# One head group per lap of TensorE's loop, kept values in the third slot, and a 28 KB ring for the weights between two layers

## The chip, the cores and the metric

The kernel runs on one core of a Trainium2 chip. TensorE (PE) multiplies matrices, VectorE (DVE), ScalarE (ACT) and GpSimd (POOL) do the rest, and SyncE (SP) issues nearly all DMAs. The core has 16 DMA engines, which serve one queue here. The metric is the device time of one execution in microseconds, the median over several.

## The reference

Two identical decode blocks follow each other, with the same weights and the same caches:

```
x = x + attention(layernorm(x))        # 2 batches, 1 query position, 512 channels
x = x + reglu(layernorm(x))            # twice, for two layers

attention: q = x @ wq                  # 32 query heads of 128
           scores = q . k_cache / sqrt(128)   # 8 key/value heads, 32768 positions
           p = softmax(scores); o = p @ v_cache; return o @ wo
reglu:     h = relu(x @ W_gate) * (x @ W_up); return h @ W_down     # 1792 hidden channels
```

All is float32. Each of the 16 pairs of batch and key/value head ("head group") has 16.8 MB of keys and 16.8 MB of values, and both layers read them all. The weights of one layer are 27.8 MB.

## The kernel before

A head group's keys and its values come as two halves each (`half`), 128 partitions by 32 blocks of 512 columns, 8.39 MB. They lie in three slots of 32 blocks in one SBUF tensor, `arena`, taken in turn (`slot`). For each block of keys `k_blocks` issues a matmul of the four query rows, padded with zeros to 32 columns (`qz`), into `pair`; for each block of values `v_blocks` issues one into `acc`. `soft_max` and `soft_tail` make the probabilities and their transpose between the two. `head_out` turns the sum of one group into columns of `oT`, and after each second group `project` multiplies by a part of `wo` (1 MB) and adds to `op`.

The order of work is written out by hand: `keys(i)` and then `values(i - 1)`, so that the softmax of group i has its keys' time and values' time to run in. Each engine works its list in order; a recorder (`Tape`) finds, for each operation, what it must wait for from the regions of `arena` and the other tensors, and sets semaphores. A load is issued by SP as soon as TensorE has used what lay at its place; loads behind it in SP's list wait with it. TensorE's list is long, so for groups 2 to 13 its instructions stand in a hardware loop of two groups a lap (`LOOPED`, `laps`); the other engines' lists are written out in full.

The second layer takes the head groups in reverse. So the last group of the first layer is the first of the second, and what is still in SBUF isn't loaded again: its two key halves and the first half of its values (`kept`), which fill the three slots.

With the slots full, all that crosses the border flows through three strips of 2048 columns behind them (`strip`): the second half of the last values (`FLOWN`), the last part of `wo`, then `wgu` (gate and up weights) in 8 loads of 896 KB, `wd` (down weights) in 6 loads, and the second layer's `wq` in 8 loads of 1 MB. `feed_forward` and `queries` do this work. The strips also hold, at other times, `wo` (`WO_AT`), the softmax's probabilities (`P_AT`), and the scaled sums (`ACS_AT`). In `queries` of the second layer the scores of the kept keys are made between the weights' matmuls, eight blocks at a time, and the next group's keys follow in three pieces (`EASED`).

At the end of the second layer the last values come in six pieces (`ENDING`), and `wo`, `wgu` (4 loads of 1.75 MB) and `wd` are loaded into free slots well before their use. The result, `xq`, is stored as 128 rows.

The profile's lines all name line 179, where the recorder calls the instruction; groups are told apart by their tiles.

Of the kernel before, what the change touches and what calls it, by code (L numbers as in the profile page):

```python
# [36 lines left out]
WO_AT, ACS_AT, MT_AT, P_AT = FLOW, FLOW + STRIP, FLOW + STRIP + D, FLOW + STRIP + 1024  # L37
PT_AT = (FLOW + 2 * STRIP, OWN)
WIDE_AT, XT_AT, SQ_AT = OWN, OWN + D, OWN + D + P
DOWN = (4, 4, 2, 2, 1, 1)  # L40
# [4 lines left out]
ENDING = ((32, 48), (48, 56), (56, 58), (58, 60), (60, 62), (62, 64))  # L45
# [8 lines left out]
class Tape:  # L54
# [28 lines left out]
    def add(self, engine, call, args, kw):  # L83
        lane = kw.pop("lane", None)
# [3 lines left out]
        ins = [a for a in (*args[1:], *kw.values()) if isinstance(a, bass.AP) and not any(a is o for o in outs)]  # L88
# [29 lines left out]
        loop = self.spot if engine == "tensor" else None  # L118
        for k, (n, other) in sorted(needs.items(), key=lambda x: -len(x[1][1].clock)):
            if loop is not None or known.get(k, 0) < n:  # L120
                op.waits[k] = n
                for e, m in ((k, n), *other.clock.items()):
                    known[e] = max(known.get(e, 0), m)
# [18 lines left out]
    def write(self):  # L142
# [66 lines left out]
        nc.sync.wait_ge(sems["out"], 16)  # L209
# [59 lines left out]
def attention_reglu_decode(nc, hold, x, k, v, wq, wo, wgu, wd, consts, out):  # L269
# [13 lines left out]
    qz = sbuf("qz", 2 * QZ).rearrange("p (a b) -> p a b", b=QZ)  # L283
# [16 lines left out]
    turn = [0, 2, 0, 0]  # L300
# [5 lines left out]
    def own(i, at):  # L306
        e = 32 + 8 * (i % 2) + 2 * at
        return stat[:, e : e + 1]

    def slot():  # L310
        turn[1] += 1
        return (turn[1] - 1) % SLOTS * ROW

    def strip():
        turn[2] += 1
        return FLOW + (turn[2] - 1) % STRIPS * STRIP

    def fetch(at, src, lane=None):
        t = arena[:, at : at + src.shape[-1]]
        if lane is None:  # L320
            lane = f"lane{turn[3] % LANES}"
            turn[3] += 1
        sp.dma_start(t, src, lane=lane)
        return t

    def half(src, n, h):
        at = slot()
        return at, fetch(at, src[n, h], f"slot{at // ROW}" if tape.spot else None)

    def spans(src, n, at, parts):  # L330
        for lo, hi in parts:
            e = at(lo) if callable(at) else at + (lo % HALF) * D
            yield lo, hi, fetch(e, src[n, lo // HALF, :, lo % HALF * D : (lo % HALF + hi - lo) * D])
# [7 lines left out]
    dve.memset(op, 0.0)  # L341

# [36 lines left out]
    def queries(L, total, first, between):  # L379
        xT, ss = centred(total)  # L380
        qp = pair2[0]
# [3 lines left out]
        if L == 0:  # L385
            whole = fetch(slot(), wq)
        for e, b in enumerate(order):
            B, kt = divmod(b, KT)
            w = fetch(strip(), wq[:, b * 4 * D : (b + 1) * 4 * D]) if L else whole[:, b * 4 * D : (b + 1) * 4 * D]
            for c in range(4):  # L390
                pe.matmul(qp[32 * c : 32 * c + 32, B, :], xT[:, kt, :], w[:, c * D : (c + 1) * D],
                          start=kt == 0, stop=kt == KT - 1)
# [4 lines left out]
            if kt == KT - 1:  # L397
                q = tile(WIDE_AT, D)
                qs = q.rearrange("p (a b) -> p a b", b=32)
                dve.transpose(q, qp[:, B, :])  # L400
                for n in range(NB):
                    dve.tensor_scalar_mul(qT[:, 16 * B : 16 * B + 16, n], qs[:, :, n], rq[:, n : n + 1])
                if B == front:
                    place_queries(0, first)

    def place_queries(i, n):
        hk, b = divmod(n, NB)
        dve.tensor_copy(qz[:, i % 2, 28 : 28 + REP], qT[:, REP * hk : REP * hk + REP, b])

    def scores(i):  # L410
        return pair2[(i + 1) % 2]

    def k_blocks(i, lo, kt):
        for at in range(kt.shape[-1] // D):
            j, ch = divmod(lo + at, 8)
            B, c = divmod(ch, 4)
            pe.matmul(scores(i)[32 * c : 32 * c + 32, B, :], qz[:, i % 2, 28 - 4 * j : 60 - 4 * j],
                      kt[:, at * D : (at + 1) * D], start=j == 0, stop=j == NT - 1)

    def soft_max(i):  # L420
        m1, nm, rs = own(i, 0), own(i, 1), own(i, 2)
# [7 lines left out]
    def soft_tail(i):  # L429
        pT, p = tile(PT_AT[i % 2], 2 * D), tile(P_AT, 2 * D)  # L430
        for B in range(2):
            dve.transpose(pT[:, B * D : (B + 1) * D], p[:, B * D : (B + 1) * D])
        pe.matmul(small[1][:, 0:1], same, own(i, 2), start=True, stop=True)
        dve.reciprocal(own(i, 3), small[1][:, 0:1])

    def v_blocks(i, lo, hi, vt, first, last):
        pT = tile(PT_AT[i % 2], 2 * D).rearrange("p (b m r) -> p b m r", m=16, r=32)
# [12 lines left out]
    def evacuate(i, split=False):  # L450
        acs = tile(PT_AT[i % 2] if split else ACS_AT, D)
        w = P if split else D
        for t in range(0, D, w):
            dve.tensor_scalar_mul(acs[:, t : t + w], acc[:, t : t + w], own(i, 3))
        return acs

    def head_out(acs, n):
        for t in range(4):
            pe.matmul(small[0][:, :REP], acs[:, t * P : (t + 1) * P], selh[:, 4 * t : 4 * t + 4], start=t == 0, stop=t == 3)
        dve.tensor_copy(oT[:, :, n % NB], small[0][:, :REP])  # L460

    def project(w, final, closing=False):
        for u in range(REP):
# [3 lines left out]
            else:  # L467
                pe.matmul(op[32 * u : 32 * u + NB, :], oT[:, u, :], rows, start=False, stop=closing)
# [6 lines left out]
    def feed_forward(L, total, ends):  # L475
        xT, ss = centred(total)
        gu = pair2[1]
        gh, hT = tile(WIDE_AT, FS), tile(XT_AT, FS)
        per = 2 if ends else 1
        for s in range(2):  # L480
            for kt in range(KT):
                b = s * KT + kt
                if b % per == 0:
                    t = fetch(ends[0] + b * F if ends else strip(), wgu[:, b * F : (b + per) * F])
                w = t[:, b % per * F : (b % per + 1) * F]
                for j in range(4):
                    pe.matmul(gu[32 * j : 32 * j + 32, s, :FS], xT[:, kt, :], w[:, j * FS : (j + 1) * FS],
                              start=kt == 0, stop=kt == KT - 1)
                if b == 0:
                    rs = factor(ss, True)  # L490
            if s == 0:
# [8 lines left out]
        for n in DOWN:  # L500
            if ends:
                at = ends[1] + c * D
            elif n == 4 or c in (8, 12):
                at = begun = strip()
            else:
                at = begun + n * D
            t = fetch(at, wd[:, c * D : (c + n) * D])
            for e in range(n):
                w = t[:, e * D : (e + 1) * D]
                if n == 4:  # L510
                    pe.matmul(dn[32 * e : 32 * e + 32, :], rows[:, c + e, :], w, start=c == 0, stop=c == 4)
                else:
                    spread(tot, rows[:, c + e, :], w, c + e == 8, c + e == NC - 1)
# [10 lines left out]
    kept = []  # L524
    for L in range(NLAYER):
        last = L == NLAYER - 1
        seq = list(range(NG)) if L % 2 == 0 else list(range(NG - 1, -1, -1))
        made = {}

        def keys(i):  # L530

            if i < NG - 1:
                place_queries(i + 1, seq[i + 1])
            at = 0
            for h in range(2):
                if last and i == 1 and h == 0:
                    parts = ((lo, t) for lo, hi, t in spans(k, seq[i], slot(), EASED))
                else:
                    parts = [(HALF * h, half(k, seq[i], h)[1])]
                for lo, t in parts:  # L540
                    for e in range(0, t.shape[-1] // D, 8):
                        k_blocks(i, lo + e, t[:, e * D : (e + 8) * D])
                        at += 1
                        if at == 2 and 1 <= i < NG - 1:
                            soft_tail(i - 1)
                        if at == 3 and i >= 2:
                            if i < NG - 1:
                                head_out(made.pop(i - 2), seq[i - 2])
                            if i % 2 == 1:
                                project(fetch(WO_AT, wo[seq[i - 2] // NB], "wo"), False, i == NG - 1)  # L550
                            if i == NG - 1:
                                head_out(made.pop(i - 1), seq[i - 1])
                                combine()
                if last and i == 1 and h == 0:
                    v_blocks(0, 0, HALF, kept[2], True, False)

        def values(i, soft):
            n = seq[i]
            for h in range(2):
                if last and i == 0 and h == 0:  # L560
                    continue
                t = half(v, n, h)[1]
                for e in range(0, HALF, 8):
                    v_blocks(i, HALF * h + e, HALF * h + e + 8, t[:, e * D : (e + 8) * D], h == e == 0, HALF * h + e == 56)
                    if soft is not None and e == 0 and h == (1 if last and i == 0 else 0):
                        soft_max(soft)
                    if i == NG - 2 and h == 0 and e == 8:
                        head_out(made.pop(i - 1), seq[i - 1])
            made[i] = evacuate(i)

        def kept_scores():
            for e in range(0, 64, 8):
                k_blocks(0, e, kept[e // HALF][:, e % HALF * D : (e % HALF + 8) * D])
                yield

        first = kept_scores() if last else iter(())
# [98 lines left out]
```

## Time and profile before

| What | Value |
|---|---|
| median of 3 runs | 2580.14 us (2574.63 to 2581.72) |
| the profiled execution | 2578.07 us, of which its span is 2576.3 us |
| TensorE busy | 51% of the span, mean granted clock 0.746 |
| VectorE, ScalarE, GpSimd busy | 6%, 2%, 0% |
| moved by DMA | 1104.94 MB, on average 429 GB/s |

How to read the lines that follow: a group line has the engine, the operation, output <- inputs, partitions x elements and how often (x), then busy time and the mean of one. A timeline line begins with start and duration in us; in brackets at its end stand the idle time before it and what ended it. A line of the chain of work that ended last has start, duration and what the time was spent on. PEld is TensorE's load of the stationary side. Every float32 matmul and its load appear as two instructions.

### The profile page before, as it was taken

Reading aid. Unit: us, or ns where it says so; the run is one execution under the profiler, and the core shown is the slowest. Engines: PE = TensorE matmul, PEld = TensorE weight load, DVE = VectorE, ACT = ScalarE, POOL = GpSimd, SP = SyncE. Lnnn points to the kernel's source line nnn. Section 1 sums busy time; section 2 is a strip of 40 time slices with the busy share of each in tenths; the row PEclk is TensorE's granted clock in tenths of the full one; section 3 lists DMA queues with packets and bytes.
Section 4 is the critical chain, followed back from the end, with each engine's and each line's share of the span. In section 5 each row is a group of like instructions: output and inputs, shape, how many; then the busy total and the mean of one; then the engine's idle time right before and its main releaser. Section 6 shows DMA issues by size and latency. Waiting matters only on the chain.

```text
span 2576.3 us, 19494 instructions
## 1 busy us (share of the span) xinstructions
PE 1308.5 (51%) x9224; PEld 333.7 (13%) x9224; DVE 147.6 (6%) x359; ACT 41.1 (2%) x67; POOL 3.0 (0%) x11
## 2 busy tenths in 40 slices
PE   2554554454455445544675455445445545554456
PEld 0111111111111111111111111111111111111111
DVE  0000000000000000000011000000000000000001
ACT  0000000000000000000000000000000000000000
POOL 0000000000000000000000000000000000000000
PEclk9777777777777777777778777777777777777777
DMA  9999999999999999999999999999999999999998
GB/s 425 425 435 438 431 431 437 431 433 432 427 440 434 431 433 430 437 434 432 403 367 434 436 429 434 434 432 435 434 430 436 430 430 439 433 432 431 433 434 368
DMA packets 27972, 1104.94 MB, mean 429 GB/s; under 512 B 3104, under 2 KB 3488, under 8 KB 6304
## 3 DMA queue, kind: packets, MB, share of 16 engines
q1 hardware_dynamic: 27648, 1104.23, 99.7%
q8 instruction: 30, 0.49, 0.1%
q10 hardware_dynamic: 288, 0.17, 0.0%
q14 instruction: 6, 0.05, 0.0%
HBM read 1104.32 MB, written 0.07 MB: 429 GB/s over the span
## 4 chain that ended last, share of the span: by engine, by line
DMA 76%; PE 20%; another core or an unknown queue 2%; SPq 1%; DVE 0%; issue 0%; ACT 0%; ACTq 0%; DVEq 0%
DMA arena<-k 44%; DMA arena<-v 27%; PE pair L179 13%; PE acc L179 5%; DMA arena<-wgu 2%; DMA cst<-consts 2%; PE small L179 1%; DMA arena<-wq 1%; SPq L179 1%; PE op L179 1%; DMA arena<-wd 0%; DMA arena<-wo 0%; DVE arena L179 0%; DVE oT L179 0%
## 5 line engine op out<-in xcount | busy, mean ns | idle before, releaser
L179 PE MATMUL acc<-arena 128*16 128x512 f32 (+1 forms) x4120 | 584.8, 723 | 603.2 <-DMA arena<-v 602.6
L179 PE MATMUL pair<-arena,qz 128*32 128x512 f32 x4096 | 596.1, 736 | 573.8 <-DMA arena<-k 573.8
L179 PEld LDWEIGHTS pair<-arena,qz 128*32 128x32 f32 x4096 | 140.7, 132 | 987.1 <-DMA arena<-k 628.8
L179 PEld LDWEIGHTS acc<-arena 128*16 128x16 f32 x4120 | 119.5, 109 | 1017.3 <-DMA arena<-v 537.5
L179 DVE TENSOR_REDUCE stat<-pair 128x1 f32<-128x1024 f32 x32 | 39.2, 1225 | 652.9 <-PE pair L179 652.9
L179 ACT ACTIVATE arena<-pair,stat 128x1024 f32<-128x1024 f32 (+1 forms) x34 | 36.9, 1086 | 2447.4 <-DVE stat L179 2364.1
L179 DVE TENSOR_SCALAR arena<-acc,stat 128x512 f32<-128x512 f32 (+1 forms) x38 | 24.8, 665 | 756.2 <-PE acc L179 756.2
L179 PE MATMUL pair<-arena 128*32 128x512 f32 (+1 forms) x256 | 44.4, 805 | 21.4 <-DMA arena<-wgu 11.5
L179 DVE STREAM_TRANSPOSE arena<-arena 128x512 f32<-128x512 f32 (+1 forms) x68 | 43.2, 671 | 5.1 <-ACT arena L179 4.9
L179 PEld LDWEIGHTS small<-cst,arena 128*128 128x128 f32 x256 | 31.2, 191 | 27.7 <-issue 25.2
L179 PE MATMUL small<-cst,arena 128*128 128x4 f32 x256 | 34.0, 256 | 1.1 <-DVE arena L179 1.1
L179 DVE RECIPROCAL stat<-small 128x1 f32<-128x1 f32 x32 | 5.2, 163 | 387.9 <-PE small L179 387.9
L179 PE MATMUL small<-stat,ones 128*128 128x2 f32 x16 | 4.5, 349 | 45.1 <-DVE stat L179 45.1
L179 DVE TENSOR_REDUCE stat<-small 128x1 f32<-128x32 f32 x32 | 6.1, 192 | 358.6 <-PE small L179 358.6
L179 PE MATMUL small<-arena,cst 128*128 128x32 f32 (+1 forms) x80 | 18.0, 342 | 7.0 <-DVE arena L179 7.0
L179 PEld LDWEIGHTS small<-arena,cst 128*128 128x128 f32 (+1 forms) x80 | 13.5, 227 | 56.7 <-issue 45.4
L179 PE MATMUL op<-arena,oT 128*2 128x512 f32 (+1 forms) x176 | 17.2, 491 | 5.3 <-DVE oT L179 4.5
L179 PE MATMUL small<-stat,cst 128*128 128x1 f32 x64 | 12.4, 264 | 3.0 <-ACT arena L179 3.0
L179 PEld LDWEIGHTS small<-stat,cst 128*128 128x128 f32 x64 | 9.7, 191 | 29.9 <-issue 26.6
L179 PEld LDWEIGHTS pair<-arena 128*32 128x32 f32 x256 | 7.2, 130 | 47.3 <-DMA arena<-wgu 24.3
L179 DVE COPY oT<-small 128x4 f32<-128x4 f32 x32 | 5.2, 163 | 140.2 <-PE small L179 140.2
L179 PE MATMUL small<-arena 128*32 128x128 f32 (+1 forms) x128 | 11.0, 486 | 3.4 <-DMA arena<-wd 2.1
(40 smaller groups left out, 56.0 us busy)
## 6 DMA issues: line engine op xcount, KB each, us to landing
arena<-wo SPq DMA_DIRECT2D x16, 1024.0 KB, 50.6
arena<-v SPq DMA_DIRECT2D x2, 4096.0 KB, 44.8
arena<-wq SPq DMA_DIRECT2D x8, 1024.0 KB, 7.5
arena<-v SPq DMA_DIRECT2D x7, 1024.0 KB, 6.3
arena<-wgu SPq DMA_DIRECT2D x8, 896.0 KB, 6.1
arena<-wgu SPq DMA_DIRECT2D x4, 1792.0 KB, 36.5
arena<-v SPq DMA_DIRECT2D x3, 2048.0 KB, 48.6
arena<-wd SPq DMA_DIRECT2D x4, 1024.0 KB, 18.8
```

Source lines behind the costliest of these rows:

```text
L179: ins = getattr(engine, op.call)(*op.args, **op.kw)
```

## The change

- TensorE's loop holds one head group a lap: groups 1 to 14 in the first layer, 2 to 15 in the second. So that every lap has the same instructions, there is one query buffer `qz`, one place for the transposed probabilities, one score buffer for all groups but the first, and `project` runs in each lap: `head_out` clears the other batch's columns of `oT` before it, and its copy into `oT` waits for the load of `wo` too. `nothing` opens and closes the sum in `op` with zeros.
- The slots X, Y, Z have fixed uses. In the first layer keys go to X and Y and values to Z and Y; in the second keys to Y and X and values to Z and X. The last groups of a layer are placed by hand.
- The last values of the first layer go to Z and the strips' area, and their last pieces to the front of Z again, over blocks already used (`FLOWN`). Both key halves stay in Y and X, and 30 blocks of values stay in Z (`KEPT`); the other 34 are loaded again (`AGAIN`).
- The weights at the border flow through one ring of 7168 columns (28 KB a partition: the strips' area and the last 1024 columns of Z). Pieces are 2 x 448 columns of `wgu` (448 KB, 16 of them), 1024 columns of `wd` (512 KB, six and two halves) and of `wq` (512 KB, 16 of them).
- At the end of the second layer `wgu` comes in pieces of 8, 8, 8, 4 and 4 units of 448 columns.
- `queries` gathers in `acc` and `op` instead of `pair`. The result is stored as 4 rows for each of the two batches, one store on SP and one on ACT.

The diff, cut to its core:

```diff
-SLOTS = 3
-FLOW = SLOTS * ROW
-STRIP = 2048
-STRIPS = 3
+X, Y, Z, FLOW = 0, ROW, 2 * ROW, 3 * ROW
-OWN = FLOW + STRIPS * STRIP
+OWN = FLOW + 6144
-LOOPED = range(2, 14)
-KEPT = ((0, 16), (16, 24), (24, 32))
-FLOWN = tuple((32 + 4 * e, 36 + 4 * e) for e in range(7)) + ((60, 62), (62, 64))
+RING = FLOW - 1024, OWN
+WO_AT = FLOW + 2048
+P_AT, ACS_AT, MT_AT = WO_AT + 2048, WO_AT + 3072, WO_AT + 3584
+PT_AT = WIDE_AT = OWN
+LAPS = range(1, 15), range(2, 16)
+FLOWN = ((0, 2, 32, Z), (0, 0, 2, RING[0]), (1, 0, 12, FLOW), (1, 12, 20, Z), (1, 20, 28, Z + 8 * D),
+         (1, 28, 30, Z + 16 * D), (1, 30, 32, Z + 18 * D))
+KEPT = ((54, 64, Z + 10 * D), (44, 54, Z), (22, 32, Z + 20 * D))
+AGAIN = ((0, 0, 22, Z), (1, 0, 12, Z + 22 * D))
+UNITS = (2,) * 16, (8, 8, 8, 4, 4)
+DOWN = (2,) * 6 + (1, 1), (4, 4, 2, 2, 1, 1)
...
-    def strip():
-        turn[2] += 1
-        return FLOW + (turn[2] - 1) % STRIPS * STRIP
+    def ring(width):
+        at = turn[1] if turn[1] + width <= RING[1] else RING[0]
+        turn[1] = at + width
+        return at
...
+                if L and c % 2 == 0:
+                    w = fetch(ring(2 * D), wq[:, at : at + 2 * D])
...
+    def head_out(n, w=None, acs=tile(ACS_AT, D)):
...
+        if w is not None:
+            dve.memset(oT[:, :, 1 - n % NB], 0.0)
+        dve.tensor_copy(oT[:, :, n % NB], small[0][:, :REP], also=() if w is None else (w,))
...
+    def nothing(start):
+        for u in range(REP):
+            pe.matmul(op[32 * u : 32 * u + NB, :], qz[:, :NB], mean_cols.to_broadcast([P, D]), start=start, stop=not start)
...
+            if e in begins:
+                n = begins[e]
+                t, at = fetch(X + e * FS if last else ring(n * FS), wgu[:, e * FS : (e + n) * FS]), e
...
+            t = fetch(Y + c * D if last else ring(n * D), wd[:, c * D : (c + n) * D])
...
+        k_at, v_at = ((X, Y), (Z, Y)) if not last else ((Y, X), (Z, X))
...
+                if h == 1 and tape.spot and i % 2 == 0 and i > 0:
+                    weights[0] = out_weights(i)
...
+        def lap(i):
+            for at in keys(i):
+                if at == 2:
+                    soft_tail()
+                if at == 3:
+                    head_out(seq[max(i - 2, 0)], weights[0])
+                    project(weights[0])
+            values(i - 1, i)
...
+            for e, (h, lo, hi, at) in enumerate(AGAIN):
+                t = part_of(v, seq[0], h, lo, hi, at)
+                if e == 0:
+                    weights = [out_weights(0)]
+                    soft_max(1)
+                    place_queries(seq[2])
+                v_blocks(HALF * h + lo, HALF * h + hi, t, False, e == len(AGAIN) - 1)
...
+        for i in tape.laps(LAPS[L], 1):
+            lap(i)
...
+            for e, (h, lo, hi, at) in enumerate(FLOWN):
+                t = part_of(v, n, h, lo, hi, at)
+                v_blocks(HALF * h + lo, HALF * h + hi, t, e == 0, e == len(FLOWN) - 1)
...
-    sp.dma_start(out, xq, lane="out")
+    for b, queue in enumerate((sp, act)):
+        queue.dma_start(out[:, b, :], bass.AP(xq.tensor, xq.offset + b * P, [[32 * P, 4], [1, P]]), lane=f"out{b}")
```

More of the change, by code (lines that the diff above doesn't have):

```diff
@@ L87, in add @@
         outs = [args[0]] + [kw[k] for k in ("accum_out",) if k in kw]
-        ins = [a for a in (*args[1:], *kw.values()) if isinstance(a, bass.AP) and not any(a is o for o in outs)]
+        ins = [a for a in (*args[1:], *kw.values(), *also) if isinstance(a, bass.AP) and not any(a is o for o in outs)]
         key = lane or engine
@@ L118, in add @@
         loop = self.spot if engine == "tensor" else None
+        here = {}
         for k, (n, other) in sorted(needs.items(), key=lambda x: -len(x[1][1].clock)):
-            if loop is not None or known.get(k, 0) < n:
+            if (known if loop is None else here).get(k, 0) < n:
                 op.waits[k] = n
+                here.update({e: max(here.get(e, 0), m) for e, m in other.clock.items()})
                 for e, m in ((k, n), *other.clock.items()):
@@ L208, in write @@
                 done = {}
-        nc.sync.wait_ge(sems["out"], 16)
+        for b in range(NB):
+            nc.sync.wait_ge(sems[f"out{b}"], 16)
         nums = sorted(s.num for s in sems.values())
@@ L380, in queries @@
         xT, ss = centred(total)
-        qp = pair2[0]
+        qp = acc, op
         rq = one()
@@ L499, in feed_forward @@
         c = 0
[L500 to L511, printed above, removed]
+        for n in DOWN[last]:
+            t = fetch(Y + c * D if last else ring(n * D), wd[:, c * D : (c + n) * D])
+            for e in range(c, c + n):
+                w = t[:, (e - c) * D : (e - c + 1) * D]
+                if e < 8:
+                    g = 32 * (e % 4)
+                    pe.matmul(dn[g : g + 32, :], rows[:, e, :], w, start=e < 4, stop=e >= 4)
                 else:
-                    spread(tot, rows[:, c + e, :], w, c + e == 8, c + e == NC - 1)
+                    spread(tot, rows[:, e, :], w, e == 8, e == NC - 1)
             c += n
@@ L563, in values @@
                 for e in range(0, HALF, 8):
[L564 to L571, printed above, removed]
+                    lo = HALF * h + e
```

270 lines of the change are left out of this document (130 added, 140 removed).

## The prediction

> **What bounds the kernel now.** I read the page first: who is busy, and who is on the chain that ended last.
>
> ```profile
> span 2576.3 us, 19494 instructions
> PE 1308.5 (51%) x9224; PEld 333.7 (13%) x9224; DVE 147.6 (6%) x359; ACT 41.1 (2%) x67; POOL 3.0 (0%) x11
> q1 hardware_dynamic: 27648, 1104.23, 99.7%
> DMA 76%; PE 20%; another core or an unknown queue 2%; SPq 1%; DVE 0%; issue 0%; ACT 0%; ACTq 0%; DVEq 0%
> ```
>
> TensorE works half of the span. One DMA queue carries 1104.23 MB with its engines taken 99.7% of the time, and three quarters of the chain are waits for it. So time is bytes over rate, plus the places where the rate drops. The rate by stage tells where those are (columns: the stretch in us, its length, busy time of each engine, granted clock, DMA share, GB/s):
>
> ```profile
> 250.30:1036.00 785.70, 391.72 (x2720) 98.82 (x2720) 40.22 (x90) 12.06 (x20) 0.00 (x0) 0.74 1.00 433
> 1242.00:1262.00 20.00, 15.13 (x104) 4.29 (x108) 3.01 (x6) 1.21 (x2) 0.00 (x0) 0.80 0.99 421
> 1262.00:1282.00 20.00, 14.34 (x92) 1.94 (x88) 0.00 (x0) 0.00 (x0) 0.00 (x0) 0.72 0.98 386
> 1282.00:1302.00 20.00, 14.40 (x108) 4.32 (x104) 2.84 (x15) 0.63 (x1) 0.56 (x1) 0.59 0.98 364
> 1302.00:1322.00 20.00, 10.71 (x102) 2.96 (x98) 3.53 (x12) 0.00 (x0) 0.00 (x0) 0.67 0.95 336
> 1322.00:1342.00 20.00, 14.72 (x98) 3.12 (x94) 1.69 (x6) 0.00 (x0) 0.70 (x1) 0.75 0.97 357
> 1342.00:1362.00 20.00, 15.68 (x144) 4.72 (x136) 4.48 (x11) 1.21 (x2) 0.00 (x0) 1.00 1.04 446
> ```
>
> Inside a layer the loop runs at 433 GB/s and nothing is to be had there. Over the border between the layers the six rows lie 12, 47, 69, 97 and 76 below that and, in the last, 13 above: 288 / 433 x 20 us = **13.3 us** lost. The DMA share stays near 1 there, so that column doesn't show the loss; GB/s does. Why the rate drops stands in the list of DMA issues (KB of one, median us from issue to landing):
>
> ```profile
> arena<-wq SPq DMA_DIRECT2D x8, 1024.0 KB, 7.5
> arena<-wgu SPq DMA_DIRECT2D x8, 896.0 KB, 6.1
> arena<-v SPq DMA_DIRECT2D x6, 512.0 KB, 45.3
> arena<-k SPq DMA_DIRECT2D x61, 48.2
> arena<-v SPq DMA_DIRECT2D x60, 48.6
> out<-xq SPq DMA_DIRECT2D x1, 64.0 KB, 1.8
> ...
> 1291.37 1.72 PE L179 MATMUL pair<-arena 128*32 128x448 f32 x8
> ```
>
> A key or value half waits 48 us in a deep queue. A border weight lands 6 to 7.5 us after its issue, because it is issued only when its strip is free. A round of the three strips is landing plus use by TensorE: 6.1 + 1.72 = 7.8 us for 3 x 0.917 MB, which is 352 GB/s, what the rows 364, 336 and 357 show.
>
> **The change part by part.** *Bytes.* Kept over the border are both key halves and 30 blocks of values where it was 32; two blocks of 256 KB, 0.52 MB at 433, cost **+1.2 us**.
>
> *The ring.* 7168 columns hold seven pieces of 1024 columns (wq, wd) or 896 (wgu) in place of three strips. What must be known is whether the round still limits. Landing is own transfer, wait behind others, and a fixed part; the fixed part is at least the 1.8 us of the output store on an empty queue, and at most a landing less its own transfer at 413 GB/s (below): 6.1 - 2.2 = 3.9 for wgu, 7.5 - 2.5 = 5.0 for wq. A piece of wgu then needs fixed + own 1.1 + half of 1.72 us on TensorE = 3.8 to 5.9 us a round, while seven pieces take 7.8 us to move; wq 5.0 + 1.3 + 1.0 = 7.3 at worst against 8.9. At both ends the queue stays fed. Then the rate is that of short rows queued behind others:
>
> ```profile
> 2534.00:2540.00 6.00, 4.68 (x48) 1.16 (x48) 0.00 (x0) 0.00 (x0) 0.00 (x0) 1.00 1.02 413
> 2543.00:2558.00 15.00, 11.14 (x92) 4.20 (x90) 2.84 (x15) 0.00 (x0) 0.55 (x1) 0.66 1.00 424
> ```
>
> The first is mostly the end's 512 KB pieces with rows of 4 KB, the second the end's wgu with rows of 14 KB. The ring's 19.40 MB (wgu 7.34, wd 3.67, wq 8.39) take 47.0 us at 413 where 433 would take 44.8: +2.2. The last values in rows of 16 and 24 KB, 28 blocks or 7.34 MB at 424: +0.3. I take 413 because rows of 3.5 and 4 KB are nearest to it; the ends are 424 (+1.0 for the ring) and the 352 of now (no gain).
>
> The Trainium skill, page "DMA: Bandwidth & Descriptors", section "Bandwidth", speaks against this: it asks for at least 1 MiB per DMA to get 75% of peak or more, and these pieces are half of that or less. At 75% of 433 the 19.40 MB would take 59.7 us, 12.7 more than I count, and the run would come out near 2583. The row of 413 doesn't agree for pieces with work queued ahead of them; for a queue that runs empty, the rows at the border do.
>
> *Where TensorE makes the ring wait.* Between the last value piece and the first release of the ring stands a chain, seen here with its ends:
>
> ```profile
> 1282.95 0.15 PEld L179 LDWEIGHTS acc<-arena 128*16 128x16 f32 x8 [0.83 <-DMA arena<-v]
> 1287.65 0.29 DVE L179 SCALAR_TENSOR_TENSOR xq<-op,xq 128x128 f32<-128x128 f32 x1 [1.72 <-PE op L179]
> 1289.20 1.72 PE L179 MATMUL pair<-arena 128*32 128x448 f32 x8 [0.35 <-DVE arena L179]
> 1307.20 0.96 PE L179 MATMUL pair<-arena 128*32 128x448 f32 x8 [2.06 <-DMA arena<-wgu]
> 1309.69 1.94 PE L179 MATMUL small<-arena 128*32 128x512 f32 x8 [1.53 <-DMA arena<-wd]
> ```
>
> When that value piece lands, wo and five wgu pieces can already be queued, since the blocks under them have been used: 1.05 + 2.29 MB, 8.1 us. The next two lie on wo, used after 4.7 us (1282.95 to 1287.65); the eighth needs the first gate matmuls, after 4.7 + 1.55 + 0.86 = 7.1, with 10.3 us of queue. With a fixed part of 1.8 to 3.9 both are short by 0 to 0.5 and 0 to 0.7. The chain behind the gate (1307.20 to 1309.69: 2.5, plus 1.0 and 3.9) has six pieces of wd over it, 7.6 us, and that before wq is shorter. I take +1.0 for all of these, near the upper sum of 1.2, since several engines must be refilled; the ends are 0 and 3. The ring together: -13.3 + 2.5 + 1.0 = **-9.8**.
>
> *Slots.* Three slots in turn become X, Y, Z, Y in the first layer and Y, X, Z, X in the second. One slot is refilled after one other load where it was two. That load now waits in SP's queue for TensorE to be through with a half that landed just before:
>
> ```profile
> 552.11 6.17 PE pair L179 x32
> 561.78 1.04 PE op L179 x8
> 562.82 1.76 PE pair L179 x16
> 564.60 47.99 DMA arena<-v
> 612.63 8.41 PE acc L179 x64
> 179.40 9.99 PE pair L179 x64
> ```
>
> The doubly used slot holds a second key half (9.99 at most) and a second value half (8.41); the first key half with the projection in it, 552.11 to 564.60, 12.5 us, lies in another slot. A half takes 8.39 MB / 433 = 19.4 us, so the refill is issued with 9.4 us of the other load ahead. Behind it on SP stand the next group's key half and, every second lap, wo; they go out at once after it with 28 us ahead. The fixed part is 5.0 at most: cost nothing, cover 4.4 us. If that went, each lost us would come twice in each of 28 laps.
>
> *One lap per loop, projection in each.* Four more projection matmuls in every second lap, 1.04 us, 14 times, and a small clear on VectorE, beside a TensorE that idles 9 us in each half: nothing; 15 us if uncovered. The copy to oT now also waits for wo, and evacuation and softmax queue behind it on VectorE; wo lands a whole key half before. One query buffer instead of two delays the second layer's first keys by the softmax chain, some 2 us, hidden by the loads ahead of them. The reload of values behind them is issued about 11 us after the first key half landed (half a half of keys, 22 kept blocks of values, at 9.4 for 32) while 19.4 us of the second move: nothing.
>
> *The end.*
>
> ```profile
> 2563.81 2.79 PE L179 MATMUL pair<-arena 128*32 128x448 f32 x16 [2.59 <-DMA arena<-wgu]
> 2567.83 3.97 PE L179 MATMUL small<-arena 128*32 128x512 f32 x32 [1.23 <-DVE arena L179]
> 2568.75 0.15 PEld L179 LDWEIGHTS small<-arena 128*32 128x32 f32 x4 [0.72 <-DMA arena<-wd]
> 2571.50 0.69 DVE L179 COPY arena<-small 128x512 f32<-128x512 f32 x1 [3.10 <-PE small L179]
> 2570.00:2576.00 6.00, 3.10 (x64) 1.61 (x56) 0.99 (x3) 0.00 (x0) 0.00 (x0) 0.91 0.10 33
> ```
>
> The last wgu load is halved, so 8 matmuls follow it instead of 16: 1.4 us sooner for the chain. But the second wd piece lands at 2568.75 and its matmuls take 1.9, so the copy can start at 2570.7 instead of 2571.5; and the last row shows wd still landing after 2570. I take **-0.8** between 0 and -1.4. The output store shrinks from 128 rows to 8 on two queues: 1.8 us were mostly fixed, so nothing, -0.2 at best.
>
> **Sum.** +1.2 - 9.8 - 0.8 = -9.4. The profiled execution took 2578.07 us, so it would take 2568.7; the median of the runs shown, 2580.14, lies 2.07 above it, which gives 2570.7, 0.36% less.
>
> **The rivals.** *The ring still starves.* If small pieces land no sooner than big ones, the border stays near 352 GB/s and the 9.8 are not won: +1.2 - 0.8, 2580.5; half of it won gives 2575.6. (The rule of the Trainium skill named above puts the run on this side.) For it speaks that packets at the border were slow while the DMA share read 0.95 and more; against it, the worst round of 7.3 us in 8.9. *Slot reuse starves the loop*, and the kernel gets slower: from the point where TensorE frees the slot later than 19.4 - 5.0 = 14.4 us after a half landed (19.4 - 1.8 at the kinder end), each late us costs 56 us; 0.5 us late gives 2570.7 + 28 = 2599. 0.17 us late already eats the gain. Against it: 10 us is the longest use seen.
>
> **How the numbers follow.** Freed in time: 0.62, with 2566 to 2575 of its own (rates 424 and 413 with the 3 us shortfall, and the tail's 0 to -1.4, and run to run spread). Ring starves in part or all: 0.25, 2573 to 2582. Loop starves: 0.13, above that. About 0.3%, 7.7 us, is what a measurement of this kernel can tell from no change; that bound lies at 2572.4, and 2570.7 is close to it. Faster 0.55 (most of the first), same 0.31 (the rest of it and most of the second), slower 0.14. The range leaves out the loop's case and a little below: 2565 to 2580.
>
> **What would show it.** After the change the queue carries 1104.75 MB; the 120 us from the landing of the first layer's last key half average 415 GB/s or more (385 now); key and value halves split into some that land about 29 us after issue and some 48; 433 stays in the loop; behind the last wgu load stand 8 matmuls. A loop under 430 GB/s, or border rows under 390, makes the prediction wrong.

## The result and the profile after

The changed kernel takes 2568.83 us (median of 7 runs, 2566.83 to 2570.02), beside 2579.37 (7 runs) for the kernel before on the same chip. The ratio is 0.9961, with a 95% interval of 0.9949 to 0.9973: 10.5 us faster. 2570.7 was forecast. The profiled execution of the changed kernel is the fastest of its seven, 2566.83 us, 2.0 below their median; that of before (2578.07) lies 1.3 below its own. They differ by 11.2 us, and the stages below account for these two.

The page of the changed kernel, in the same lines as before:

```profile
span 2565.0 us, 19871 instructions
PE 1319.8 (51%) x9384; PEld 344.1 (13%) x9384; DVE 148.8 (6%) x390; ACT 41.1 (2%) x67; POOL 2.9 (0%) x11
q1 hardware_dynamic: 29672, 1104.69, 99.9%
q8 instruction: 17, 0.28, 0.0%
...
DMA 74%; PE 24%; another core or an unknown queue 1%; issue 0%; SPq 0%; DVE 0%; ACTq 0%; DVEq 0%
...
arena<-wq SPq DMA_DIRECT2D x16, 512.0 KB, 7.8
arena<-wgu SPq DMA_DIRECT2D x16, 448.0 KB, 7.6
...
arena<-k SPq DMA_DIRECT2D x61, 45.2
arena<-v SPq DMA_DIRECT2D x59, 47.6
```

The queue carries 0.46 MB more (0.52 was forecast), and TensorE does more work; still the run is shorter, so the queue must have run faster somewhere. The weights' pieces are half as large and land a little later after their issue (7.6 us for wgu, 6.1 before): more of them wait in the queue, and that is what keeps it full. One line moved that the prediction did not look at: the queue that fetches instructions. It had, in the kernel before:

```profile
q8 instruction: 30, 0.49, 0.1%
```

The rate by stage in the changed kernel (columns as in the prediction):

```profile
250.00:1036.00 786.00, 395.98 (x2756) 100.96 (x2744) 40.22 (x99) 12.05 (x20) 0.00 (x0) 0.74 1.00 433
1242.00:1262.00 20.00, 12.34 (x80) 3.48 (x84) 3.01 (x6) 1.21 (x2) 0.00 (x0) 0.67 0.96 412
1262.00:1282.00 20.00, 15.56 (x128) 4.00 (x124) 0.00 (x0) 0.00 (x0) 0.00 (x0) 0.86 0.99 415
1282.00:1302.00 20.00, 15.67 (x120) 4.47 (x108) 2.85 (x15) 0.63 (x1) 0.56 (x1) 1.00 1.02 397
1302.00:1322.00 20.00, 14.97 (x110) 3.75 (x112) 3.86 (x14) 0.00 (x0) 0.70 (x1) 1.00 1.03 407
1322.00:1342.00 20.00, 19.19 (x164) 6.27 (x160) 2.84 (x8) 0.00 (x0) 0.00 (x0) 1.00 1.04 430
1342.00:1362.00 20.00, 15.26 (x132) 4.81 (x136) 2.91 (x7) 1.21 (x2) 0.00 (x0) 0.91 1.06 455
1242.00:1362.00 120.00, 93.00 (x716) 26.77 (x720) 15.47 (x49) 3.04 (x5) 1.26 (x2) 0.91 1.02 419
```

The loop still moves 433 GB/s. The border went from a mean of 385 to 419; against 433 it now loses 14 / 433 x 120 = 3.9 us where it lost 13.3. That is 9.4 us of the gain. The rows that were worst, 336 and 357 at 1302 to 1342, are 407 and 430.

Inside the loop, the chain of work that ended last shows the slots' new use:

```profile
505.24 30.04 DMA arena<-v
...
535.31 9.72 PE acc L188 x64
...
545.05 28.92 DMA arena<-k
...
574.01 9.16 PE pair L188 x64
```

The load of 28.92 us is issued at 545.05, the moment that TensorE is through with the half before it (535.31 + 9.72), and lands in time for the queue to stay at 433.

Two more places gave something. One is the loops, in the bytes that the queue moved in two fixed stretches, 60 to 1242 us and 1362 to 2500 us (MB in the third column), first of the kernel before, then of the changed one:

```profile
q1 hardware_dynamic: 9682, 511.41, 100.1%
...
q1 hardware_dynamic: 9337, 492.90, 100.2%
```

```profile
q1 hardware_dynamic: 9686, 512.01, 100.2%
...
q1 hardware_dynamic: 9606, 492.70, 100.1%
```

Together 1004.31 and 1004.71: 0.40 MB more in the same time, about 0.9 us at 433. The other is the end of the data, 6 us taken at the same distance from the last addition, before and after:

```profile
2566.35:2572.35 6.00, 4.33 (x40) 1.29 (x40) 2.30 (x5) 0.00 (x0) 0.00 (x0) 0.60 0.41 162
```

```profile
2555.00:2561.00 6.00, 5.17 (x44) 1.57 (x48) 0.87 (x2) 0.00 (x0) 0.00 (x0) 0.50 0.72 285
```

The mean busy share of the 16 DMA engines is 0.72 there after the change and 0.41 before it: when the queue has nothing more to start, some of them finish before others, and in this execution of the kernel before they finished less evenly. That is (285 - 162) / 433 x 6 = 1.7 us.

The sum for the two profiled executions: border -9.4, bytes +0.46 / 433 = +1.1, loops -0.9, last data -1.7: -10.9 of the 11.2 measured. 0.3 us is not assigned.

### The profile page after: what moved, and what is told of

Same layout as the page of the kernel before. It is cut to its first block, busy times and chain, and to the rows that moved or that the text cites. A ratio compares the mean times of both kernels' runs of the same rounds, so it can differ in the third digit from the quotient of the medians.

```text
span 2565.0 us, 19871 instructions
## 1 busy us (share of the span) xinstructions
PE 1319.8 (51%) x9384; PEld 344.1 (13%) x9384; DVE 148.8 (6%) x390; ACT 41.1 (2%) x67; POOL 2.9 (0%) x11
## 3 DMA queue, kind: packets, MB, share of 16 engines
q1 hardware_dynamic: 29672, 1104.69, 99.9%
## 4 chain that ended last, share of the span: by engine, by line
DMA 74%; PE 24%; another core or an unknown queue 1%; issue 0%; SPq 0%; DVE 0%; ACTq 0%; DVEq 0%
DMA arena<-v 35%; DMA arena<-k 35%; PE acc L188 12%; PE pair L188 12%; DMA cst<-consts 2%; DMA arena<-wd 1%; DMA arena<-wgu 0%; PE small L188 0%; PE op L188 0%; DMA arena<-wq 0%; SPq L188 0%; DVE arena L188 0%; DVE xq L188 0%; DVE stat L188 0%
## 5 line engine op out<-in xcount | busy, mean ns | idle before, releaser
L188 PE MATMUL acc<-arena 128*16 128x512 f32 (+1 forms) x4200 | 597.4, 721 | 600.5 <-DMA arena<-v 599.7
L188 PEld LDWEIGHTS pair<-arena,qz 128*32 128x32 f32 x4096 | 148.0, 131 | 973.0 <-issue 706.7
L188 PEld LDWEIGHTS acc<-arena 128*16 128x16 f32 (+1 forms) x4200 | 123.2, 110 | 1020.2 <-DMA arena<-v 655.4
L188 PE MATMUL op<-arena,oT 128*2 128x512 f32 (+1 forms) x296 | 32.9, 533 | 9.9 <-DVE oT L188 9.9
L188 PE MATMUL pair<-arena 128*32 128x448 f32 x128 | 21.7, 603 | 7.1 <-DMA arena<-wgu 6.3
L188 PE MATMUL op<-arena 128*32 128x512 f32 x64 | 11.7, 598 | 1.8 <-DMA arena<-wq 1.5
```

The costliest lines, as they stand in the source:

```text
L188: ins = getattr(engine, op.call)(*op.args, **op.kw)
```

## Experiments

### The ring: how many pieces it holds

Theory: what the border loses is set by whether a piece's round (fixed part of the landing, own transfer, TensorE's use of it) is shorter than the transfer of all the pieces in the ring. Rival: the gain comes from other parts of the change, and the ring's form matters little. Three kernels, all from the changed one. The small value piece that lay in the ring's first columns stays where it was, outside the smaller ring.

Three pieces of the old size in the old 6144 columns:

```diff
-RING = FLOW - 1024, OWN
+RING = FLOW, OWN
...
-UNITS = (2,) * 16, (8, 8, 8, 4, 4)
-DOWN = (2,) * 6 + (1, 1), (4, 4, 2, 2, 1, 1)
+UNITS = (4,) * 8, (8, 8, 8, 4, 4)
+DOWN = (4, 4, 2, 2, 1, 1), (4, 4, 2, 2, 1, 1)
...
-                    w = fetch(ring(2 * D), wq[:, at : at + 2 * D])
+                    w = fetch(ring(4 * D), wq[:, at : at + 4 * D])
...
```

> The kernel after with one thing undone: the border ring has 6144 columns and big pieces again (wgu 1792 columns, wq 2048, wd as at the end), so three pieces as the strips had; slots, loop and kept blocks stay. Theory (the round of the ring is what was won): landing 6 to 7.5 us plus use 1 to 2 us for three pieces, back to about 350 GB/s; the 120 us at the border lose some 13 us instead of 3.9, and the time is about 2578. Rival (the gain comes from the loop, the slots or the end): stays within 2 us of 2568.8.

Six small pieces in the same 6144 columns:

```diff
-RING = FLOW - 1024, OWN
+RING = FLOW, OWN
...
```

> The kernel after with a ring of 6144 columns instead of 7168, small pieces: six instead of seven. Theory: six pieces of wgu move in 6.7 us and of wq in 7.6, a round is 3.8 to 5.9 and at most 7.3, so it is still fed; only the two hand-overs (project, first gate matmuls) have 1.1 us less ahead of them: 0.5 to 2 us more than after, 2569.3 to 2571. Rival (area counts in proportion): a seventh of the way back, the same number, so this run only bounds; a result over 2573 would say that the ring is at its edge.

Four small pieces in 4096 columns:

```diff
-RING = FLOW - 1024, OWN
+RING = FLOW + 2048, OWN
...
```

> The kernel after with a ring of 4096 columns, small pieces: four. Four pieces of wgu move in 4.4 us, of wq in 5.1. With a fixed part of landing of 3.9 to 5 us the round (5.9 to 7.3) is longer than that and wgu runs at about 75% of the rate of now: 16 wgu and 16 wq pieces lose 0.4 and 0.5 us each, and the hand-over after wo, with two wgu pieces behind it instead of five, 3 us: 2568.8 + 14 + 3 = 2580 to 2586. With a fixed part of only 1.8 the round (3.8, 4.1) still fits and only the hand-over costs: 2570 to 2572.

Measured, against before on the same chip (2579.07): three large pieces 2576.83 us (ratio 0.999, 0.9981 to 0.9999), six small 2571.03 (0.9968, 0.9956 to 0.998), four small 2584.91 (1.0024, 1.0015 to 1.0033). The 120 us of the border, of three large, six small and four small pieces:

```profile
1242.00:1362.00 120.00, 83.83 (x632) 22.97 (x636) 15.48 (x49) 3.04 (x5) 1.26 (x2) 0.76 0.95 381
```

```profile
1242.00:1362.00 120.00, 90.66 (x716) 25.68 (x720) 15.47 (x49) 3.04 (x5) 1.26 (x2) 0.94 1.01 416
```

```profile
1242.00:1362.00 120.00, 87.46 (x585) 22.78 (x585) 13.73 (x44) 1.84 (x3) 1.26 (x2) 0.82 0.91 343
```

Seven small pieces against six are worth some 2 us (2.2 between the medians, but the two intervals overlap); the size of a piece in the same area is worth 5.8 (2576.83 - 2571.03); with four small pieces the kernel is slower than before the change. So the ring's form carries 8.0 of the 10.5 us. The rival keeps the rest: with three large pieces the border is as slow as before the change, 381 GB/s beside 385, and the kernel is still 2.2 us faster.

The landing of a `wgu` piece in the kernel with four:

```profile
arena<-wgu SPq DMA_DIRECT2D x16, 448.0 KB, 4.5
```

Less 1.1 us for its own transfer that leaves at most 3.4 for the fixed part, an estimate within the 1.8 to 3.9 that the prediction gave wgu. The round, 4.5 us and TensorE's use of the piece (0.94 us for one at 1300.88), is some 5.4 us, longer than the 4.4 in which four pieces move at 413: this ring starves, as the theory says. Its slowest rows, 260 GB/s at 1282 to 1302 and 286 at 1302 to 1322, also hold the hand-overs from wo to wgu and from wgu to wd; how much of the loss belongs to each was not separated.

The Trainium skill, page "DMA: Bandwidth & Descriptors", section "Bandwidth", asks for 1 MiB per DMA; here, in the same columns, the pieces of up to 1 MB are the slow ones, 381 GB/s at the border beside 416. The trace disagrees with that rule for pieces that have others queued ahead of them.

### The ring alone, in the kernel before

Everything else of the change is left out: three slots in turn, two laps a loop, 32 kept blocks, 6144 columns.

```diff
-    def strip():
-        turn[2] += 1
-        return FLOW + (turn[2] - 1) % STRIPS * STRIP
+    def strip(width):
+        at = turn[2] if turn[2] + width <= OWN else FLOW
+        turn[2] = at + width
+        return at
...
-DOWN = (4, 4, 2, 2, 1, 1)
+DOWN = (2,) * 6 + (1, 1), (4, 4, 2, 2, 1, 1)
...
+                if L and c % 2 == 0:
+                    w = fetch(strip(2 * D), wq[:, at : at + 2 * D])
...
+                    if not ends and j % 2 == 0:
+                        t = fetch(strip(2 * FS), wgu[:, b * F + j * FS : b * F + (j + 2) * FS])
...
```

> The kernel before with one part of the change alone: its 6144 columns of strips become a ring with small pieces (wgu 896 columns, wq and wd 1024), values still in pieces of four blocks, 32 blocks of values kept; slots, loop and end as before. Theory: the border's loss falls from 13.3 to about 5, and the two blocks are not loaded again (-1.2 against after): about 2571 to 2572, where before has 2579.4. Rival (the new loop and slots bring the gain): stays near 2579.

2573.84 us (0.9977, 0.9968 to 0.9986): 5.2 faster than before, where 7 to 8 were expected: a miss. The profiled execution (2576.09, a long one of its runs) has 359 and 309 GB/s at 1262 to 1302, where 386 and 364 were, and then 379 and 409, where 336 and 357 were. Over the whole border it comes to this:

```profile
1242.00:1362.00 120.00, 90.06 (x624) 24.54 (x624) 15.54 (x50) 3.04 (x5) 1.26 (x2) 0.84 0.98 387
```

That is 0.6 us better than the 385 of before. In this execution the ring cures the later rows, and the hand-over from the values to the weights loses nearly as much again. The times say that the ring alone is worth 5.2 us; where the shorter runs won them, this profile doesn't show. Together with the 381 of three large pieces it does show that neither the small pieces alone nor the rest of the change alone brings the border far, and that both together do (416 in the same 6144 columns).

### The last values through the ring

The changed kernel again, with the ring of 6144 columns, but all 32 blocks kept and the last values flowing through the ring. Its first load there is 12 blocks in one piece, where the kernel before has pieces of four. It moves 0.52 MB less than its partner with six pieces.

```diff
...
-FLOWN = ((0, 2, 32, Z), (0, 0, 2, RING[0]), (1, 0, 12, FLOW), (1, 12, 20, Z), (1, 20, 28, Z + 8 * D),
-         (1, 28, 30, Z + 16 * D), (1, 30, 32, Z + 18 * D))
-KEPT = ((54, 64, Z + 10 * D), (44, 54, Z), (22, 32, Z + 20 * D))
-AGAIN = ((0, 0, 22, Z), (1, 0, 12, Z + 22 * D))
+FLOWN = ((0, 0, 32, Z), (1, 0, 12, FLOW), (1, 12, 16, FLOW), (1, 16, 20, FLOW + 4 * D), (1, 20, 24, FLOW + 8 * D),
+         (1, 24, 28, FLOW), (1, 28, 30, FLOW + 4 * D), (1, 30, 32, FLOW + 6 * D))
+KEPT = ((0, 32, Z),)
+AGAIN = ((1, 0, 32, Z),)
...
```

> The kernel after, but the first layer's last values flow through the ring's 6144 columns as before (12 blocks, then pieces of 4 and 2 over blocks just used), and Z keeps the whole first half (32 blocks); the ring has six small pieces as in the run with six. Theory formed on the ring alone in the kernel before, which won 5 us and not 8: the place of the last values matters, because wo and the first wgu pieces may only be issued when the values they lie on are used, and those land last; 3 to 6 us more than the run with six pieces (2571.0), less 1.2 for two blocks: 2573 to 2576. Rival (what was missing there was the loop and the slots): 2571.0 - 1.2, about 2570.

2576.92 us (0.9993, 0.9984 to 1.0002), 5.9 more than with six pieces and the values in Z, and 7.1 with the 1.2 us of bytes that it saves. Two stretches, and the first issues of SyncE for `wo` and the gate weights, with the values in the ring:

```profile
1262.00:1282.00 20.00, 15.60 (x108) 2.90 (x104) 0.00 (x0) 0.00 (x0) 0.00 (x0) 0.76 0.70 278
1282.00:1302.00 20.00, 14.43 (x104) 5.34 (x96) 2.84 (x15) 0.00 (x0) 0.56 (x1) 0.63 0.91 321
...
1283.51 0.33 SPq L188 DMA_DIRECT2D arena<-wo  x1
1287.54 11.71 SPq L188 DMA_DIRECT2D arena<-wgu  x8
```

and the same issues in the changed kernel:

```profile
1269.89 0.33 SPq L188 DMA_DIRECT2D arena<-wo  x1
1270.58 23.85 SPq L188 DMA_DIRECT2D arena<-wgu  x16
```

With the values over old blocks in Z the ring is free 13.6 us earlier for wo, and 17 us earlier for wgu, while values are still on their way. That is the cover that the prediction counted as "wo and five wgu pieces can already be queued".

But the 7.1 us are not what this cover brought over the kernel before. Most of them are one hole that this run has and the kernel before has not:

```profile
1266.00:1274.00 8.00, 7.35 (x68) 1.61 (x60) 0.00 (x0) 0.00 (x0) 0.00 (x0) 0.99 0.26 84
...
1261.32 12.04 PE L188 MATMUL acc<-arena 128*16 128x512 f32 x88 [6.50 <-DMA arena<-v]
```

TensorE waits for the kept half until 1261.32 and works through its 32 blocks first. So SyncE can issue the next piece of values only at 1271.71, when the 12 blocks have landed, and the queue has had nothing to do: (433 - 84) / 433 x 8 = 6.4 us. In the same 8 us the kernel before moved 371 GB/s, and the kernel with six pieces 420. A fairer measure is the ring alone in the kernel before against six small pieces in the changed one, in the same 6144 columns: 2573.84 - 2571.03 = 2.8 us for all the rest of the change, 4.0 when the 1.2 us of bytes are set aside. Some 1 to 2 us of this are the loops' (see the section on instructions), so the values' place is worth 2 to 3 us, an estimate; the small pieces are worth 5.2 in the one kernel and 5.8 in the other.

### Slot reuse: how far is the cover

The prediction costed the double use of a slot at nothing, with 9.4 us of other work ahead of the refill. To reach its limit, TensorE does useless matmuls before the last eight blocks of each doubly used half, 16, 24 or 32 of them, into `pair2[0]`, a place in PSUM that nothing reads then. No part of the computation is left out.

```diff
+    def idle_work(t):
+        for e in range(16 if tape.spot else 0):      # 24, 32
+            c = e % 4
+            pe.matmul(pair2[0][32 * c : 32 * c + 32, 0, :], same[:, :32], t[:, :D], start=True, stop=True)
...
+                        if h == 1 and e == 24:
+                            idle_work(t)
...
+                    if lo == 56:
+                        idle_work(t)
```

> The kernel after with 16 useless matmuls of a key block's size, into a PSUM bank that the loop leaves free, ahead of the last 8 blocks of the second key half and the second value half of every looped lap: the doubly used slot comes free some 4.7 us later (0.147 us an instruction, two for a matmul), 14.6 us after its half landed instead of 9.9. Lead of the refill 4.8 us. Theory (a refill needs 1.8 to 3.9 us of other load ahead of it): no loss, within 3 us of 2568.8. If the fixed part is 5 or more: 56 us for each missing us.

> The same with 24 matmuls: free 17 us after landing, lead 2.4 us. With a fixed part of 1.8 no loss; with 3 us 34 us more; with 3.9, 84 us more.

> The same with 32 matmuls: free 19.3 us after landing, lead 0.1 us: the whole fixed part is lost 56 times, 95 us (1.8) to 213 us (3.9) more than 2568.8. From this run and the one before the fixed part is read.

One execution each: 2568.27, 2576.93 and 2611.5 us, beside the 2568.8 without them. The chain with 24 (first row, a key half) and with 32 (a value half and a key half), and the loop's rate with 32:

```profile
574.51 13.98 PE pair L188 x112
```

```profile
545.03 7.53 PE acc L188 x48
552.56 6.87 PE pair L188 x64
559.42 1.77 PE acc L188 x16
...
585.49 16.43 PE pair L188 x128
...
407.00:1036.00 629.00, 413.30 (x3188) 109.54 (x3184) 30.34 (x77) 9.65 (x16) 0.00 (x0) 0.82 0.99 427
```

With 16, use takes some 13 us and nothing is lost. With 24 it takes 14.0 to 15.1, leaves 4.3 to 5.4 of 19.4 us, and the run is 8.1 us longer. Not all of that is the refills': the border, where no useless matmul stands, ran at 407 GB/s in this execution where 419 were, which is 3.3 us. The two stretches of 60 to 1242 and 1362 to 2500 us moved 2.85 MB less than in the changed kernel, 6.6 us or 0.12 for each of 56 refills, but 5.5 us of it fell into the second layer, and why there isn't known. (The two profiled executions differ by 10.1 us.) With 32 it takes 16.2 to 16.4 in these rows and leaves 3.0 to 3.2; 42.7 us, 0.76 for each, with 426 and 425 GB/s in the two stretches. The expectation for 32 was far above that because it took a useless matmul for slower than it was: 6.87 us for 64 instructions, 0.107 each. So the rival's mechanism exists, with its edge between 14 and 16 us of use, where the prediction had 14.4 to 17.6; the kernel stands at 8.5 to 10. A refill needs some 3.0 + 0.76 = 3.8 us of other work ahead of it to land without a gap, an estimate from the run with 32, one execution.

### Fewer instructions to fetch

The instruction queue went from 30 packets to 17. Theory: each packet takes room from the data, so the shorter list of TensorE is part of the gain. Rival: fetches of 0.28 MB cost their share of the bytes, under 1 us in all. The first eight, or the first three, laps of each layer's loop are written out, with the same work.

```diff
...
-        for i in tape.laps(LAPS[L], 1):
+        for i in LAPS[L][:8]:                        # 3
+            lap(i)
+        for i in tape.laps(LAPS[L][8:], 1):
             lap(i)
```

> The kernel after with the first 8 laps of each layer written out instead of looped: no work changes, TensorE's program is longer. The instruction queue should go from 17 packets to about 50. Theory (part of the gain that the border doesn't explain is fewer instruction loads on the DMA engines: before had 30 packets): the bytes cost 1.3 us and each packet holds up one of 16 engines, so that landings spread more; 2571 to 2574. Rival (instruction loads are free): 2568.8, within 1 us.

> The kernel after with the first 3 laps of each layer written out, about as many groups outside loops or doubled in them as the kernel before has. Eight laps a layer took the instruction queue from 17 to 52 packets and cost 7.0 us, 0.2 us a packet. Theory: about 30 packets as in the kernel before, 13 x 0.2 = 2.6 us more, 2571.4; that is then the part of the gain that the border doesn't explain. Rival (the eight laps disturbed the border alone): within 1 us of 2568.8.

With eight laps written out there are 52 packets, and the run takes 2575.79 us (0.9989, 0.998 to 0.9998), 7.0 more than the changed kernel. With three there are 30, as many as before the change: 2570.96 (0.997, 0.9958 to 0.9981), 2.1 more, with an interval that overlaps that of the changed kernel. The bytes moved in the same two stretches as above, with eight:

```profile
q8 instruction: 52, 0.85, 0.1%
...
q1 hardware_dynamic: 9670, 511.52, 100.1%
...
q1 hardware_dynamic: 9528, 492.06, 100.0%
```

1003.58 MB, 1.13 less than the changed kernel, or 2.6 us; with three 0.53 less, 1.2 us. That is 0.07 to 0.09 us a packet, about two times its share of the bytes (16 KB at 433: 0.038). The changed kernel is a low one of its kind, though: it and the six others with 17 packets and the same loops (three large, six and four small pieces, values in the ring, the two of the next section) moved 1004.71 to 1005.21 MB in these stretches, and the three kernels with 30 packets (before, the ring alone in it, three laps) 1004.09 to 1004.31. Between the means, 1004.97 and 1004.19, lie 1.8 us, or 0.14 a packet. The rest of the 7.0 lies outside the loops: at the border (403 GB/s, where 419 were) and in the last data (161 GB/s over the last 6 us). So the theory holds in the loops, with 1 to 2 us for 13 packets. Why the border is slower too, although as many packets fall into it, is open.

### The end

The last wgu load whole again (16 matmuls behind it), and, as the other way round, wd in small pieces, for the case that the end hangs on its last piece:

```diff
-UNITS = (2,) * 16, (8, 8, 8, 4, 4)
+UNITS = (2,) * 16, (8, 8, 8, 8)
```

> The kernel after with the last wgu load of the second layer in one piece of 8 units again. The prediction's term says 0.8 us later from the landing of the last wgu piece to the end; the trace of after (second wd piece landing 5.3 us behind it, the same 9.8 us to the last addition as before) says 0 to 0.3. To be read in the profile, not in the time.

```diff
-DOWN = (2,) * 6 + (1, 1), (4, 4, 2, 2, 1, 1)
+DOWN = (2,) * 6 + (1, 1), (2,) * 6 + (1, 1)
```

> The kernel after with wd of the second layer in pieces of 2 blocks (six, then two of 1), as in the first, instead of 4, 4, 2, 2, 1, 1. If the end hangs on the landing of the second wd piece, the matmuls of its first half now run while the rest is on its way: the copy 0.7 to 1 us earlier and the time about 2568. Rival (the end hangs on the last wd piece): no change, and more small rows, +0.1.

2568.76 (one execution) and 2568.68 us (0.996, 0.9946 to 0.9974): neither moves the time. The end of the changed kernel, from the landing of the last wgu load to the last addition:

```profile
2552.41 0.96 PE L188 MATMUL pair<-arena 128*32 128x448 f32 x8 [1.23 <-DMA arena<-wgu]
...
2557.73 2.79 PE L188 MATMUL small<-arena 128*32 128x512 f32 x24 [0.57 <-DMA arena<-wd]
...
2559.80 0.69 DVE L188 COPY arena<-small 128x512 f32<-128x512 f32 x1 [4.62 <-PE small L188]
...
2562.26 0.29 DVE L188 SCALAR_TENSOR_TENSOR xq<-small,xq 128x128 f32<-128x128 f32 x1 [1.77 <-PE small L188]
```

and the last addition in the kernel before:

```profile
2573.61 0.29 DVE L179 SCALAR_TENSOR_TENSOR xq<-small,xq 128x128 f32<-128x128 f32 x1 [1.42 <-PE small L179]
```

From landing to addition it was 2573.61 - 2563.81 = 9.80 us, and is 9.85; with the load whole 9.74. TensorE is through with the eight matmuls 0.96 us after the landing, where sixteen took 2.79, and then waits for wd, whose second piece lands 5.3 us after the last wgu load (4.9 before). So the halving is worth nothing. With small wd the last matmuls wait for the last wd piece until 2563.93, 0.5 us before the last addition at 2564.43: the rival of that expectation. With the load whole, the last data empties at 277 GB/s, as evenly as in the changed kernel, so the 1.7 us there don't come from the halving either; nor do they follow the packets of instructions alone, for the ring in the kernel before (30 packets) empties at 276 and three laps written out (30) at 273. What makes the engines finish unevenly in some runs was not tried.

## Why the prediction was right, point by point

- **The ring, -9.8.** Right in mechanism and size: -9.4 in the profiled execution (13.3 to 3.9). The rate taken for short rows, 413, lies between the 397 and 430 of the three rows that hold the ring. The two rows of the last values, 412 and 415, lose 1.8 us where 0.3 was taken for their shorter rows, and the last row, 455, gives 1.0 back. The shortfall at the hand-over was taken as +1.0 between 0 and 3. In the changed kernel it is seen in the row of 397: (413 - 397) / 433 x 20 = 0.7. But it isn't the same in each execution. The kernel with small wd at the end, equal at the border, has there:

```profile
1282.00:1302.00 20.00, 16.05 (x100) 5.42 (x100) 2.79 (x15) 0.64 (x1) 0.56 (x1) 0.74 0.97 357
```

This is 1.8 us more, and 411 over the whole border. The granted clock beside it is 0.74 where it was 1.00; yet with 16 useless matmuls the row reads 394 at a clock of 0.83, and with the last load whole 358 at 0.83, so the clock doesn't settle it. The border's gain, ring and values' place together, is thus some 7 to 9.4 us.
- **Bytes, +1.2.** 1104.69 MB, +0.46: +1.1. Right.
- **The end, -0.8.** Wrong: nothing. The step that failed is "8 matmuls follow it instead of 16: 1.4 us sooner for the chain"; the sentence behind it, that the second wd piece bounds the copy, was the whole truth, since that piece didn't land sooner either.
- **What was costed at nothing.** Slot reuse: right, with its edge measured between 14 and 16 us. The projection in each lap and the wait for wo on VectorE: right, 433 in the loop and the same chain of halves. One query buffer and the reload: no row shows a loss, the last border row reads 455.
- **What was left out.** The fetching of instructions, some -1 us in the loops (up to -1.8 by the kernels beside), and the more even finish, -1.7 in these two executions, together -2.6, against the -0.8 at the end that didn't come. So the profiled execution is 1.9 us below the 2568.7 forecast for it, and the median 1.9 below 2570.7. The even finish is, as far as is known, luck of these two executions: the same end in the ring alone emptied at 276. The total came near because the ring is most of it; the small terms partly cancel.
- **The rivals.** "The ring still starves" is what happens with three large pieces (2576.8) or four small ones (2584.9), not with seven. "Slot reuse starves the loop" happens 4 us of use or more further on. The border above 415, the loop at 433, halves landing at 29 us beside others near 47, and eight matmuls behind the last wgu load are all there as "what would show it" asked.

## What to carry to other kernels

Where one queue bounds a kernel, look for the stretches in which its GB/s drops while its DMA share stays near 1: there a ring of few large pieces is refilled too late. Compare a piece's round (fixed part of the landing, own transfer, use) with the time to move all the pieces of the ring; in the same memory, smaller pieces shorten the first and leave the second as it is. And make room early, by putting the last values over blocks already used, so that the weights' ring is free while values are still landing: the small pieces were worth 5 to 6 us here, and this an estimated 2 to 3.

## What the runs showed of the hardware

- A packet of instructions (16 KB) takes 0.07 to 0.14 us from a full queue, two to four times its share of the bytes (0.038), and writing eight laps of each loop out made the kernel 7.0 us slower though the engine that runs them is half idle. The Trainium skill, page "Runtime: NRT & Kernel Launch", section "Instruction fetch mechanics", counts fetches as hidden by the pace of instructions and says that kernels prefer full unrolling; the engine's own wait was not measured here, but for this kernel, bound by its queue, the runs don't agree that unrolling is to be preferred.
- A store on an empty queue landed in 1.8 us, but a refill under a full queue needs some 3.8 us of work ahead of it (an estimate from the run with 32 useless matmuls, where 3.0 to 3.2 were left and 0.76 us was lost each time).
- The same border ran at 419, 411 and 411 GB/s in profiled executions of kernels that are equal up to there (the changed one, the last load whole, small wd at the end). The cause stays open.
